# B's output weights in five pieces instead of seven, and the kept sums placed ahead of the last four rows

## The chip, the cores and the metric

The kernel runs on one core of one Trainium2 chip. The metric is the time of one execution on the device, in microseconds (us). Of the kernel before, three runs are shown: 1324.14 us is their median, 1324.11 the lowest and 1324.51 the highest. A profile of one more execution gives the trace that the text reads.

The engines are named as in the profile: PE is TensorE (PEld its weight loads), DVE is VectorE, ACT is ScalarE, POOL is GpSimd, SP is SyncE, which here issues nearly all DMAs. A name with a q (SPq, PEq) is that engine's sequencer.

## The reference

Two attention blocks, A and B, are computed for one new token of each of 2 sequences, and are mixed by a gate. Each has 32 heads of width 128 and a cache of 4096 keys and values for each head, all in float32; x is 2 x 512.

```python
def attend(x, k_cache, v_cache, wq, wo):             # once for A, once for B; both with A's x
    q = heads(x @ wq)                                # 512 -> 32 heads of 128
    p = softmax(einsum("bhqd,bhkd->bhqk", q, k_cache) * 128 ** -0.5)
    o = einsum("bhqk,bhkd->bhqd", p, v_cache)
    return flat(o) @ wo                              # 4096 -> 512
g = sigmoid((x * gate_w).sum(-1, keepdims=True))
out = g * attend(A) + (1 - g) * attend(B)
```

Nearly all of the data are the four caches, 128 MB each, of which every byte is used once. The output weights `wo` are 8 MB for A and 8 MB for B.

## The kernel before, in words

**The long part.** The work is cut into 32 units (A and B, eight groups of four heads, two sequences). A unit is 8 MB of keys and 8 MB of values. VectorE multiplies keys by the query and sums (L392, L395), ScalarE takes the exponentials (L367), and TensorE multiplies them with the values into the PSUM tile `vp` (L371). Keys go to two tiles `kt0` and `kt1`, values to one tile `vt`. Each engine runs its own loop, and semaphores written by hand tie the loops together. SP issues the loads in a fixed order, each one when its tile has become free. This part isn't changed.

**The end.** Three tiles are used again there. The last values go to `kt0`. A's output weights go to `vt` when the values before them have been used (L248). B's output weights go to `kt1` when the last keys have been used (L251). In both, a partition holds 32 rows of 512 numbers (`OR` = 32 rows of 2 KB, so a row of all 128 partitions is 256 KB). Row r of the output product is one matmul of a 128 x 2 column of `on` (the weighted and gated heads) with a 128 x 512 row of the weights. 32 rows of A and 32 of B are summed.

**How the rows are summed.** Rows go round over four strips of the PSUM tile `most`: row r adds to partitions 32s and 32s + 1, with s = r % 4 (`project_out`, L460 to L468). So `most` holds four partial sums, a strip each. This is done for all rows of A and rows 0 to 23 of B (`EARLY` = 24). ScalarE then copies `most` to the SBUF tile `kept` (L582).

The last eight rows of B go another way (`project_last`, L478 to L481): each is cut into four column ranges of 128, one for each strip, and these four matmuls add into four PSUM banks (`qa0`, `qa1`, `vp`, `bank`). The four partial sums of `kept` are folded into the same four banks by four matmuls with the matrix `fold` (L586), which adds the strips up. Then each bank holds a finished quarter of the output. Two engines copy the quarters, and two DMAs store the halves (L593 to L601).

**The order.** TensorE works strictly in the order of the program: A's rows, B's rows 0 to 23, rows 24 to 27 in the strips, the fold, rows 28 and 29, row 30, row 31 in two halves. Before a row with which a piece of the weights begins it waits for that piece (`arrived`; each piece has a semaphore of its own). A weight row here is one program instruction and appears in the trace as two matmuls and two weight loads, two passes of a float32 product.

**The pieces.** B's output weights are loaded in seven DMAs, on SP's queue one behind the other: rows 0 to 15, 16 to 23, 24 to 27, 28 and 29, 30, and the two halves of row 31 (L252, L253).

Of the kernel before, what the change touches and what calls it, by code (L numbers as in the profile page):

```python
# [13 lines left out]
B = 2  # L14
# [13 lines left out]
STRIPS = P // QT  # L28
OR = H * DH // P
DQ = DH // OR  # L30
EARLY = OR - 8
PAD = 72
NP = 2 * NG
SCALE = DH ** -0.5
# [13 lines left out]
class Streams:  # L48
# [32 lines left out]
    def put(self, e, make, reads=(), writes=(), gives=None):  # L81

        self.before(e, reads, writes)
        i = make(self.engines[e])
        if gives is not None:
            i.then_inc(gives, 1)
            return None
        self.ticks[e] += 1
        i.then_inc(self.sems[e], 1)
        point = self.sems[e], self.ticks[e]  # L90
        self.after(point, reads, writes)
        return point
# [51 lines left out]
def tile_gated_decode(ctx: ExitStack, tc: tile.TileContext, ins: dict, out: bass.AP):  # L144
# [14 lines left out]
    fold = small.tile([P, B], F32, name="fold")  # L159
# [22 lines left out]
    with tc.tile_critical(no_gpsimd_drain=True):  # L182
        S = Streams(nc, tc)
        put, take = S.put, S.take
# [26 lines left out]
        def load_parts(item, t, src, slots, *cuts):  # L211
            parts[item] = [S.dma("sp", t[:, i:j], src[:, i:j], slot=s) for s, i, j in zip(slots, cuts, cuts[1:])]

        def arrived(e, item, *which):
            p = parts[item]
            S.wait(e, [p[k] for k in which] if which else p)
# [27 lines left out]
        def load_wo(n):  # L244
            t = wo[n]
            src = ins[n + "_wo"].rearrange("(p r) e -> p r e", p=P)
            if n == "A":
                nc.sync.wait_ge(v_free, NU - 1)  # L248
                load_parts(("wo", n), t, src, "f", 0, OR)
                return  # L250
            nc.sync.wait_ge(k_free[1], NU // 2)  # L251
            load_parts(("wo", n), t, src, "abchi", 0, OR // 2, EARLY, OR - 4, OR - 2, OR - 1)  # L252
            parts["wo", n] += [S.dma("sp", t[:, OR - 1, h], src[:, OR - 1, h], slot=s) for s, h in zip("jk", HALVES)]  # L253

        wo = {n: t.rearrange("p r d -> p (r d)").rearrange("p (r e) -> p r e", e=D) for n, t in (("A", vt), ("B", kt[1]))}
# [10 lines left out]
        start = Scratch(kt[1]).take  # L266
# [191 lines left out]


        def project_out(k, n, *rows_):  # L460
            bounds = (0,) if n == "A" else (0, OR // 2)
            for r in range(*rows_):
                if r in bounds:
                    arrived("pe", ("wo", n), bounds.index(r))
                s = r % STRIPS
                put("pe", lambda x: x.matmul(most[s * QT:s * QT + B], on[:, k, r], wo[n][:, r],  # L466
                                             start=n == "A" and r < STRIPS, stop=n == "B" and r >= EARLY - STRIPS),
                    [r_on], [r_most])  # L468
# [5 lines left out]
        def strips(*which):  # L474
            for s in which or range(STRIPS):
                yield s, r_acc[s], acc[s][s * QT:s * QT + B, :W], slice(s * W, (s + 1) * W)

        def project_last(part, r, *which):  # L478
            arrived("pe", ("wo", "B"), part)
            for _, a, t, e_ in strips(*which):  # L480
                put("pe", lambda x: x.matmul(t, on[:, 1, r], wo["B"][:, r, e_], start=r == EARLY, stop=r == OR - 1), [r_on], [a])  # L481


        projections()
# [24 lines left out]
        for u in range(2, NU):  # L509
            load_k(u)  # L510
            load_v(u - 1)
        load_v(NU - 1)
        load_wo("A")
        load_wo("B")

        exps(0, 0, 0, lambda make, gives: put("act", make, [r_nm[0], r_sc, r_pad, r_lp, r_nil], [], gives))
# [16 lines left out]
        sums, turned, laid, outs, kept = end(2 * B * P), end(D), end(P), end(P), end(D)  # L533
        drawn, onp = end(D), end(2 * OR * B)
        on = onp.rearrange("p (n r b) -> p n r b", n=2, b=B)
        totals = [end(D // 2)[:B] for _ in HALVES]
        r_sums, r_drawn, r_turned, r_laid, r_outs, r_kept = R(), R(), R(), [R() for _ in range(2 * B)], R(), R()
# [8 lines left out]
        for j in range(STRIPS):  # L546
# [3 lines left out]
                start=True, stop=True), [r_pick, r_vs], [r_heads])  # L550
# [27 lines left out]
        r_on.writers = [point]  # L578

        project_out(0, "A", OR)  # L580
        project_out(1, "B", EARLY)
        put("act", lambda x: x.activation(kept, most, AF.Copy), [r_most], [r_kept])  # L582
        for r in range(EARLY, OR - 4):
            project_last(2, r)
        for _, a, t, e_ in strips():
            put("pe", lambda x: x.matmul(t, fold, kept[:, e_], start=False, stop=False), [r_fold, r_kept], [a])  # L586
        for r in range(OR - 4, OR - 2):
            project_last(3, r)
        project_last(4, OR - 2)
        project_last(5, OR - 1, 0, 1)  # L590
        project_last(6, OR - 1, 2, 3)

        for h, e in enumerate(("sp", "act")):  # L593
            copied, r_total = sem(f"copied{h}"), R()
            for i in range(2):
                _, a, t, _ = next(strips(2 * h + i))
# [28 lines left out]
```

## Time and profile before

| | |
|---|---|
| median of the runs shown (lowest to highest) | 1324.14 us (1324.11 to 1324.51) |
| span of the profiled execution, first to last instruction | 1322.3 us |
| DVE busy | 1165.3 us, 88% |
| PE busy | 331.7 us, 25% |
| ACT busy | 100.7 us, 8% |
| read from HBM, mean rate over the span | 570.43 MB, 431 GB/s |
| B's output weights: issue of the seven pieces begins | 1276.14 us |
| last matmul begins | 1319.23 us |

The runs' own time for the profiled execution is not listed beside its span. The span leaves out what lies ahead of the first instruction and behind the last, and the median of the runs is 1.8 us above it. Times in the text such as 1309.28 are us from the span's start. The matmuls' ends are modelled by the profiler. A timeline row gives start, duration, engine, line, operation, out and in, a count of merged instructions, and in brackets the idle time before and what ended it. In a row of a DMA the last number is the time from its issue to its landing. The granted clock (PEclk) is the share of TensorE's full clock that the chip's throttle let through.

### The profile page before, as it was taken

To read this page: it belongs to the slowest core of one execution; us is meant where nothing else is said; L and a number is where in the kernel's file an instruction comes from. 1 tells how busy PE (TensorE), PEld (TensorE's weight loads), DVE (VectorE), ACT (ScalarE), POOL (GpSimd) and SP (SyncE) were. 2 spreads that over 40 slices of the span, in tenths; PEclk is the share of its full clock that TensorE was granted. 3 is DMA by queue.
4 is the path that set the end of the run, shared out by engine and by line. 5 is a ranking of instruction groups with operands and counts; after the bars stand their busy time and mean duration, and the time that the engine had idled before them with its cause. 6 is when DMAs were issued, how large, how long until landed. Compare 5 with 4: busy or idle time off the path is not lost. (4 is left out here: it accounts for less than half of the span.)

```text
span 1322.3 us, 6216 instructions
## 1 busy us (share of the span) xinstructions
PE 331.7 (25%) x2382; PEld 90.3 (7%) x2382; DVE 1165.3 (88%) x316; ACT 100.7 (8%) x328; POOL 0.7 (0%) x6
## 2 busy tenths in 40 slices
PE   3112222211222221122222122222212322311256
PEld 0000000000000000000000000000000000000011
DVE  1978999999999999999999999999999999999961
ACT  0000100001010000101000010100001010000100
POOL 0000000000000000000000000000000000000000
PEclk9566666556666655666665666666556666555678
DMA  9999999999999999999999999999999999999998
GB/s 404 453 412 443 442 416 442 442 416 442 442 418 442 440 436 424 442 440 418 442 440 418 442 442 416 442 442 424 436 442 436 422 442 440 418 442 442 417 442 352
DMA packets 10820, 570.51 MB, mean 431 GB/s; under 512 B 1207, under 2 KB 1467, under 8 KB 1726
## 3 DMA queue, kind: packets, MB, share of 16 engines
q1 hardware_dynamic: 10804, 570.43, 99.6%
q8 instruction: 3, 0.05, 0.0%
q14 instruction: 3, 0.02, 0.0%
q10 hardware_dynamic: 10, 0.01, 0.0%
HBM read 570.43 MB, written 0.00 MB: 431 GB/s over the span
## 5 line engine op out<-in xcount | busy, mean ns | idle before, releaser
L392 DVE TENSOR_TENSOR kt<-kt,q 128x16384 f32<-128x16384 f32 x31 | 534.0, 17226 | 71.3 <-DVEq L97 71.3
L395 DVE TENSOR_REDUCE sc<-kt 128x128 f32<-128x16384 f32 x31 | 533.8, 17220 | 1.1
L371 PE MATMUL vp<-vt,pr 128*32 128x512 f32 x1984 | 283.1, 734 | 915.5 <-PEq L97 915.5
L371 PEld LDWEIGHTS vp<-vt,pr 128*32 128x32 f32 x1984 | 77.9, 132 | 1120.7 <-issue 1120.7
L367 ACT ACTIVATE pr<-sc,nm 32x128 f32<-32x128 f32 x128 | 50.9, 398 | 108.1 <-ACTq L97 102.8
L430 ACT ACTIVATE pr<-nil 128x512 f32<-128x512 f32 x31 | 19.3, 623 | 456.8 <-ACTq L97 456.8
L451 ACT ACTIVATE vs<-vp,slot 128x128 f32 x15 | 5.5, 368 | 448.1 <-ACTq L97 448.1
L337 PE MATMUL qa<-vt,cols 128*2 128x512 f32 x128 | 18.4, 739 | 39.9 <-PEq L97 39.9
L367 ACT ACTIVATION_READ_ACCUMULATOR pr<-sc,nm (+1 forms) x128 | 23.5, 184 | 0.0
L416 DVE SCALAR_TENSOR_TENSOR vs<-vp,slot,vs 128x128 f32 x45 | 15.8, 351 | 8.6 <-DVEq L97 7.6
L599 DVE COPY kt<-qa 2x128 f32<-2x128 f32 x1 | 0.3, 278 | 23.8 <-PE qa L481 23.8
L352 DVE STREAM_TRANSPOSE vt<-vt 128x1024 f32<-128x1024 f32 x2 | 2.4, 1224 | 17.1 <-ACT vt L348 17.1
L498 DVE TENSOR_REDUCE sc<-kt 128x64 f32<-128x8192 f32 x2 | 17.4, 8686 | 0.1
L496 DVE TENSOR_TENSOR kt<-kt,q 128x8192 f32<-128x8192 f32 x2 | 17.4, 8688 | 0.0
L455 ACT ACTIVATE vp<-nil 128x512 f32<-128x512 f32 x15 | 9.0, 600 | 99.2 <-ACTq L97 99.2
L544 DVE SCALAR_TENSOR_TENSOR vs<-vp,slot,vs 128x128 f32<-128x128 f32 x3 | 1.1, 351 | 12.9 <-ACT vs L542 12.8
L371 PE MATMUL vp<-kt,pr 128*32 128x512 f32 x64 | 9.0, 724 | 10.9 <-DMA kt<-in_B_v_cache_dram 10.9
L466 PE MATMUL most<-vt,kt 128*2 128x512 f32 x64 | 9.6, 765 | 6.5 <-DMA vt<-in_A_wo_dram 6.5
L400 DVE TENSOR_REDUCE rm<-sc 128x1 f32<-128x128 f32 x31 | 8.7, 281 | 2.3
L406 DVE STREAM_TRANSPOSE q<-qsel 128x128 f32<-128x128 f32 x30 | 9.3, 311 | 1.0
L289 DVE COPY cols<-bank 128x8 f32<-128x8 f32 x1 | 0.2, 167 | 10.0 <-PE bank L287 10.0
L401 DVE STREAM_TRANSPOSE across<-rm 128x32 f32<-128x32 f32 x31 | 6.6, 212 | 1.1
(73 smaller groups left out, 60.4 us busy)
## 6 DMA issues: line engine op xcount, KB each, us to landing
kt<-in_A_k_cache_dram SPq DMA_DIRECT2D x2, 4096.0 KB, 35.6
kt<-in_B_wo_dram SPq DMA_DIRECT2D x1, 4096.0 KB, 33.1
kt<-in_B_wo_dram SPq DMA_DIRECT2D x1, 2048.0 KB, 37.6
kt<-in_B_wo_dram SPq DMA_DIRECT2D x1, 1024.0 KB, 39.5
kt<-in_B_wo_dram SPq DMA_DIRECT2D x1, 512.0 KB, 40.3
vt<-in_A_v_cache_dram SPq DMA_DIRECT2D x16, 28.5
kt<-in_B_k_cache_dram SPq DMA_DIRECT2D x16, 42.6
kt<-in_B_wo_dram SPq DMA_DIRECT2D x1, 256.0 KB, 40.4
```

The source lines that it names most:

```text
L337: last = nc.tensor.matmul(t[h * QT:h * QT + B], cols[:, c], blocks[:, c, i, h], start=c == 0, stop=c == KC - 1)
L367: do(lambda x: x.activation(padded[h, :, b, j * VC:(j + 1) * VC], s[h].rearrange("p (c a) -> p c a", a=VC), AF.Exp, bias=m[h], accum_out=l ...
L371: return x.matmul(vp[c % STRIPS * QT:(c % STRIPS + 1) * QT], padded[:, c].rearrange("p b m -> p (b m)"), t[:, c * VC:(c + 1) * VC].rearran ...
L392: at = D_.do(lambda x: x.tensor_tensor(kt[o], kt[o], q[:, None, :].to_broadcast([P, NS, DH]), op=ALU.mult), after)
L395: at = D_.do(lambda x: x.tensor_reduce(sc[o], kt[o], axis=AX.X, op=ALU.add), at)
L406: return D_.do(lambda x: x.transpose(q, qsel[:, 0].to_broadcast([P, DH // QT, QT])), at)
L416: at = D_.do(lambda x: x.scalar_tensor_tensor(vs[:, g], vp[:, a * DH:(a + 1) * DH], slot[:, a:a + 1], vs[:, g], op0=ALU.mult, op1=ALU.add) ...
L430: return A_.do(lambda x: x.activation(padded[:, :, b], nil[:, :, None].to_broadcast([P, NVC, G * VC]), AF.Copy))
L455: A_.do(lambda x: x.activation(vp, nil.to_broadcast([P, VC * DH]), AF.Copy))
L466: put("pe", lambda x: x.matmul(most[s * QT:s * QT + B], on[:, k, r], wo[n][:, r], start=n == "A" and r < STRIPS, stop=n == "B" and r >= EA ...
L496: put("dve", lambda x: x.tensor_tensor(t, t, q[:, None, :].to_broadcast([P, NS // 2, DH]), op=ALU.mult), [r_q], [r])
L498: put("dve", lambda x: x.tensor_reduce(sc[0][:, h * NS // 2:(h + 1) * NS // 2], t, axis=AX.X, op=ALU.add), [r], [R()])
```

## The change

B's output weights come in five pieces: rows 0 to 21, rows 22 to 27, rows 28 to 30, and the two halves of row 31. Rows 0 to 27 of B, four more than before, go into `most`, and only the last four rows go into the strips. `kept` is folded into the four banks first, ahead of rows 28 to 31, and starts their sums (`start=True`), so the strip matmuls of the rows no longer start any. What is computed is the same.

```diff
-EARLY = OR - 8
+FIRST = OR - 10
+EARLY = OR - 4
@@ load_wo
-            load_parts(("wo", n), t, src, "abchi", 0, OR // 2, EARLY, OR - 4, OR - 2, OR - 1)
+            load_parts(("wo", n), t, src, "abc", 0, FIRST, EARLY, OR - 1)
             parts["wo", n] += [S.dma("sp", t[:, OR - 1, h], src[:, OR - 1, h], slot=s) for s, h in zip("jk", HALVES)]
@@ project_out
-            bounds = (0,) if n == "A" else (0, OR // 2)
+            bounds = (0,) if n == "A" else (0, FIRST)
@@ project_last
-                put("pe", lambda x: x.matmul(t, on[:, 1, r], wo["B"][:, r, e_], start=r == EARLY, stop=r == OR - 1), [r_on], [a])
+                put("pe", lambda x: x.matmul(t, on[:, 1, r], wo["B"][:, r, e_], start=False, stop=r == OR - 1), [r_on], [a])
@@ the end of the program
         project_out(0, "A", OR)
         project_out(1, "B", EARLY)
         put("act", lambda x: x.activation(kept, most, AF.Copy), [r_most], [r_kept])
-        for r in range(EARLY, OR - 4):
+        for _, a, t, e_ in strips():
+            put("pe", lambda x: x.matmul(t, fold, kept[:, e_], start=True, stop=False), [r_fold, r_kept], [a])
+        for r in range(EARLY, OR - 1):
             project_last(2, r)
-        for _, a, t, e_ in strips():
-            put("pe", lambda x: x.matmul(t, fold, kept[:, e_], start=False, stop=False), [r_fold, r_kept], [a])
-        for r in range(OR - 4, OR - 2):
-            project_last(3, r)
-        project_last(4, OR - 2)
-        project_last(5, OR - 1, 0, 1)
-        project_last(6, OR - 1, 2, 3)
+        project_last(3, OR - 1, 0, 1)
+        project_last(4, OR - 1, 2, 3)
```

Two places show how the order of instructions moves. Lines of the changed kernel are one higher up to its last loop (L466 becomes L467, L481 becomes L482), and the fold is L585. On TensorE, after A's rows, the kernel before has this; `kt_86` holds B's weights, `kt_85` holds `on` and `kept`, `landed_a` to `landed_c` are the semaphores of the first three pieces, and `done_act` is ScalarE's:

```order
L466 MATMUL most<-kt_86,kt_85 2x512 [waits landed_a]
L466 MATMUL most<-kt_86,kt_85 2x512 x15
L466 MATMUL most<-kt_86,kt_85 2x512 [waits landed_b]
L466 MATMUL most<-kt_86,kt_85 2x512 x7
L481 MATMUL qa_89<-kt_86,kt_85 2x128 [waits landed_c]
```

The changed kernel has there:

```order
L467 MATMUL most<-kt_86,kt_85 2x512 [waits landed_a]
L467 MATMUL most<-kt_86,kt_85 2x512 x21
L467 MATMUL most<-kt_86,kt_85 2x512 [waits landed_b]
L467 MATMUL most<-kt_86,kt_85 2x512 x5
L585 MATMUL qa_89<-kt_85,fold 2x128 [waits done_act]
```

Behind the first wait stand 22 rows instead of 16, and behind the last row into `most` comes a wait for ScalarE's copy instead of one for a piece of the weights. On SP's queue, behind A's output weights, the changed kernel has these loads of B's, and the store of the first half (sizes are partitions x numbers):

```order
L107 DMA vt<-in_A_wo_dram 128x16384
L107 DMA kt_86<-in_B_wo_dram 128x11264
L107 DMA kt_86<-in_B_wo_dram 128x3072
L107 DMA kt_86<-in_B_wo_dram 128x1536
L107 DMA kt_86<-in_B_wo_dram 128x256 x2
L107 DMA out_dram<-kt_85 2x256
```

Before, five loads of 8192, 4096, 2048, 1024 and 512 numbers stood in place of the three ahead of the two halves.

## The prediction

> **What bounds the kernel now.** I read the page first, then the DMA issues with their landings, then the last 25 us in order of time. The page's slices:
>
> ```profile
> span 1322.3 us, 6216 instructions
> PEclk9566666556666655666665666666556666555678
> DMA  9999999999999999999999999999999999999998
> DMA kt<-in_B_wo_dram 3%; DVE kt L392 1%; DVE sc L395 1%; PE qa L481 0%; SPq L106 0%; PE vp L481 0%; ACT kt L598 0%; PE qa L586 0%; PE bank L481 0%; DVEq L134 0%; PE bank L586 0%; PE vp L586 0%
> ```
>
> The DMA engines are busy in every slice, so the kernel ends when the last bytes have come and what hangs on them is done. The chain that ended last says the same of its last stretch: it is the load of B's output weights (3%), with some matmuls behind it. All that the change touches lies there. The loads and the issuing queue:
>
> ```profile
> kt<-in_B_wo_dram SPq DMA_DIRECT2D x1, 4096.0 KB, 33.1
> kt<-in_B_wo_dram SPq DMA_DIRECT2D x1, 2048.0 KB, 37.6
> kt<-in_B_wo_dram SPq DMA_DIRECT2D x1, 1024.0 KB, 39.5
> kt<-in_B_wo_dram SPq DMA_DIRECT2D x1, 512.0 KB, 40.3
> kt<-in_B_wo_dram SPq DMA_DIRECT2D x1, 256.0 KB, 40.4
> kt<-in_B_wo_dram SPq DMA_DIRECT2D x2, 128.0 KB, 39.9
> ```
> ```profile
> 1276.14 3.44 SPq L106 DMA_DIRECT2D kt<-in_B_wo_dram  x7
> ```
>
> The seven pieces are issued by 1279.6 and land from 1309.24 (1276.14 + 33.1) on. Now the end of the timeline, TensorE and ScalarE (start, duration, engine, line, operation, and in brackets the idle time before):
>
> ```profile
> 1299.47 9.58 PE L466 MATMUL most<-vt,kt 128*2 128x512 f32 x64 [6.49 <-DMA vt<-in_A_wo_dram]
> 1309.28 3.61 PE L466 MATMUL most<-kt,kt 128*2 128x512 f32 x32 [0.23 <-DMA kt<-in_B_wo_dram]
> 1314.13 1.90 PE L466 MATMUL most<-kt,kt 128*2 128x512 f32 x16 [1.23 <-DMA kt<-in_B_wo_dram]
> 1316.17 0.60 ACT L582 ACTIVATE kt<-most 128x512 f32<-128x512 f32 x1 [23.42 <-PE most L466]
> 1316.57 0.28 PE L481 MATMUL qa<-kt,kt 128*2 128x128 f32 x2 [0.55 <-DMA kt<-in_B_wo_dram]
> ...
> 1317.55 0.28 PE L586 MATMUL qa<-kt,fold 128*2 128x128 f32 x2
> ...
> 1319.11 0.09 PEld L481 LDWEIGHTS vp<-kt,kt 128*2 128x2 f32 x2 [0.30 <-DMA kt<-in_B_wo_dram]
> ...
> 1319.23 0.27 PE L481 MATMUL bank<-kt,kt 128*2 128x128 f32 x1
> ```
>
> At each piece TensorE is found waiting for a DMA, and after the last one (1319.11) only 0.39 us of matmuls follow, to 1319.50. The copy of `most` (L582, 0.60 us) lies wholly beside the wait for row 28 and the matmuls of rows 24 to 27. So the end is set by arrival: 16 rows take 9.81 us (1299.47 to 1309.28), the next 16, in six pieces, 9.83 (to 1319.11). That is 0.613 us a row, whatever the piece.
>
> **The price of a row on TensorE.** A row is one product, shown as two matmul records. Its pace is read from the weight loads, four in a group, two rows:
>
> ```profile
> 1300.28 0.15 PEld L466 LDWEIGHTS most<-vt,kt 128*2 128x2 f32 x4 [0.70 <-issue]
> 1301.14 0.15 PEld L466 LDWEIGHTS most<-vt,kt 128*2 128x2 f32 x4 [0.71 <-issue]
> ...
> 1305.02 0.10 PEld L466 LDWEIGHTS most<-vt,kt 128*2 128x2 f32 x4 [0.33 <-issue]
> 1305.45 0.10 PEld L466 LDWEIGHTS most<-vt,kt 128*2 128x2 f32 x4 [0.33 <-issue]
> ```
>
> 0.86 us for two rows early, 0.43 later: 0.43 and 0.214 us a row. The granted clock is the reason, seen in stretches of 3.4 us (columns: length; busy us of PE, PEld, DVE, ACT, POOL; granted clock; DMA):
>
> ```profile
> 1297.79:1301.19 3.40, 1.72 (x12) 0.31 (x16) 0.00 (x0) 0.00 (x0) 0.00 (x0) 0.50 0.92 390
> 1301.21:1304.60 3.39, 3.39 (x24) 0.56 (x20) 0.00 (x0) 0.00 (x0) 0.00 (x0) 0.50 0.92 396
> 1304.62:1308.02 3.40, 3.40 (x37) 0.73 (x32) 0.00 (x0) 0.00 (x0) 0.00 (x0) 1.00 1.01 434
> 1308.03:1311.43 3.40, 3.17 (x33) 0.62 (x29) 0.00 (x0) 0.00 (x0) 0.00 (x0) 1.00 0.98 419
> ...
> 178.23:181.62 3.39, 2.68 (x16) 0.82 (x20) 3.39 (x1) 0.00 (x0) 0.00 (x0) 0.50 1.11 483
> 181.64:185.03 3.39, 3.39 (x40) 1.02 (x36) 3.39 (x1) 0.00 (x0) 0.00 (x0) 1.00 0.98 425
> ...
> 1144.20:1147.60 3.40, 2.58 (x16) 0.73 (x20) 3.40 (x1) 0.00 (x0) 0.00 (x0) 0.50 0.76 328
> 1147.61:1151.00 3.39, 3.39 (x22) 0.88 (x18) 3.39 (x1) 0.00 (x0) 0.00 (x0) 0.50 1.34 580
> ...
> 727.77:731.17 3.40, 1.41 (x16) 0.21 (x8) 3.40 (x1) 0.63 (x1) 0.00 (x0) 1.00 0.89 386
> 731.18:734.58 3.40, 0.00 (x0) 0.00 (x0) 3.40 (x1) 0.00 (x0) 0.00 (x0) 1.00 0.76 328
> 734.60:738.00 3.40, 0.00 (x0) 0.00 (x0) 1.64 (x6) 1.69 (x7) 0.00 (x0) 0.50 1.34 578
> ...
> 843.82:847.22 3.40, 1.37 (x16) 0.17 (x8) 3.40 (x1) 0.89 (x2) 0.00 (x0) 1.00 0.80 347
> 847.24:850.64 3.40, 0.00 (x0) 0.00 (x0) 3.40 (x1) 0.00 (x0) 0.00 (x0) 0.50 0.76 328
> ```
>
> In these rows the clock changes only between windows of 3.41 us on a fixed grid. It is raised after a window with 2.68 us of matmuls or more, not after 2.58. It falls after one with 1.37 us or less, and is kept after 1.41.
>
> **The change, part by part.** *Fewer pieces.* Seven DMAs become five. Their issue (3.44 us for seven, so 0.5 each) ends 30 us before the first lands: nothing on the path. Nor do bytes come sooner: the last 16 rows in six pieces took 0.02 us longer than 16 rows in one. I bound this edit by -0.15 (all of the 0.30 us wait that the last half row shows, halved) and 0, and take 0.
>
> *The first piece has 22 rows.* It lands at the row pace at 1309.28 + 6/8 of the 4.85 us to 1314.13, so 1312.9. Until then TensorE, done with A at 1309.05, has nothing: 3.9 us idle instead of 0.23. Sixteen rows that were done at 1312.89 are now only begun.
>
> *Four more rows go to `most`.* At full clock 28 rows take 28 x 0.214 = 5.98 us, to 1318.9; with 0.19 us of drain (1.90 - 8 x 0.214) to 1319.1. The pieces of rows 22 to 27 (1316.6) and 28 to 30 (1318.4) have by then landed, or nearly.
>
> *The kept sums first.* The copy of `most` now stands between the 28 rows and the strips, whose first matmuls wait for it; rows 28 to 31 queue behind that wait, in order. Its cover is gone: 0.14 us to its start (1316.03 to 1316.17), 0.60, and some 0.06 to TensorE, so 0.80. Then five steps over the strips, of two passes each: ten passes ran from 1316.57 to 1317.55, 0.109 apart, so 9 x 0.109 + 0.27 = 1.25 us. End of the matmuls: 1319.07 + 0.80 + 1.25 = 1321.1, against 1319.50. Even at full clock that is **+1.6 us**; the copies and the store behind it stay as they are.
>
> *The clock.* The idle 3.9 us now meets the gate. With this execution's grid, the window 1308.03 to 1311.44 would hold matmuls only to 1309.05, 1.0 us, under 1.37: half clock from 1311.44. The 22 rows start at half. The window to 1314.86 has 1.95 us, too little; the next is full; full clock from 1318.27. So 5.4 us at half speed, costing half of that: +2.7, together **+4.3 us**. The grid need not fall so in another execution, so I bound it. Where the clock is at half when the rows start, the half-speed stretch lasts from 2.68 us to 2.68 + 3.41 = 6.09, which costs 1.3 to 3.0. Where the window around A's end still held 1.41 us, the fall comes up to 1.3 us into the rows, and then a whole window runs at half: 1.7. Moving the grid through 3.41 us in small steps and following these rules, the sum lies between +2.9 and +4.6, with its middle at +3.8, which I take.
>
> The Trainium skill, page "TensorE: Matmul & The Clock Gate", section "What's actually happening", lets the clock fall after at least one idle window of about 3.4 us. Taken to the letter, a gap of 3.9 us holds a whole idle window in only 0.5 of 3.41 positions, and mostly the clock would stay: +1.6. The trace disagrees: a window with 1.37 us of matmuls in it was enough (843.82).
>
> **From trace to run.** The sums are differences within an execution of 1322.3 us of span; the runs' median, 1324.14, has 1.8 us more outside it, which I carry over. +3.8 gives 1327.9.
>
> **Rivals.**
> 1. *The clock stays full over the gap.* +1.6, 1325.7. For it: 1312.89 to 1314.13 was bridged, and after 727.77 a whole empty window was. Against: it needs over 1.37 us of matmuls in every window around 3.9 us of nothing. 0.13.
> 2. *Arrival still sets the end,* as before, and the two saved pieces bring it forward: 1324.0, not slower. It decides if TensorE is done with 28 rows, copy and strips by 1319.5: (1319.5 - 1312.9 - 0.19 - 0.80 - 1.25) / 28 = 0.156 us a row. The quickest rows here take 0.214, in the sixteen that had all landed as well. 0.04.
> 3. *The clock never rises again before the end.* 28 rows at 0.43 instead of 0.214 cost 6.0, ten passes at 0.218 1.1: +8.7, 1332.8. It would need a window full of these matmuls that does not raise the clock; that of 1301.21 did. 0.03.
> 4. *The change does not do what it says.* The recorded order shows the 28 rows and the early kept sums, so this has no chance of its own.
>
> **How the numbers follow.** The forecast, half clock for part of the rows, has 0.80; it alone gives 1327.0 to 1328.8, with 0.2 either way for what I left at nothing. Rival 1 is next and lies below, so the range goes from 1325.6 to 1329.0. About 0.2% (2.65 us) is what a measurement of this kernel can tell from no change; the limit is 1326.8. The forecast's lower end comes within 0.3 of it, so I give 0.06 of its chance to no change, and with rival 1 and half of rival 2: slower 0.77, the same 0.21, faster 0.02.
>
> **What would show it.** Right: the group of `most` matmuls on B's weights has some 3.9 us of DMA wait in one piece before it and starts near 1312.9; the granted clock reads 0.50 in a stretch after that; the first strip matmul waits for ScalarE's copy of `most`; the chain's end runs through TensorE and that copy, with the last half row landed 2 us or more before its matmul. Runs whose grid lies otherwise differ by up to 1.7 us, more than the 0.4 of before. Wrong: 1.00 in all these windows (rival 1), a first piece that lands well before 1312.9, or a last strip that still waits for a DMA (rival 2).

## The result, and the profile after

The changed kernel takes 1327.65 us (median of 8 runs, 1327.18 to 1328.36), the kernel before in the same session 1324.11 (8 runs, 1323.96 to 1324.51). The ratio is 1.0027 with a 95% interval of 1.0018 to 1.0036: 3.5 us slower. The profiled execution took 1327.85 us, of which its span is 1326.1, so 1.8 us lie outside the span, as before.

The page of the changed kernel: the span, and the chain that ended last, by line. It now runs through the products into `most` (L467) and ScalarE's copy of it (L583), which did not appear in it before:

```profile
span 1326.1 us, 6166 instructions
DMA kt<-in_B_wo_dram 3%; DVE kt L393 1%; DVE sc L396 1%; PE most L467 1%; PE qa L482 0%; ACT kt L583 0%; ACT kt L596 0%; PE qa L585 0%; PE bank L482 0%; PE vp L482 0%; DVEq L135 0%; PE bank L585 0%; PE vp L585 0%
```

The loads of B's output weights, with KB and us from issue to landing:

```profile
kt<-in_B_wo_dram SPq DMA_DIRECT2D x1, 5632.0 KB, 36.6
kt<-in_B_wo_dram SPq DMA_DIRECT2D x1, 1536.0 KB, 39.9
kt<-in_B_wo_dram SPq DMA_DIRECT2D x1, 768.0 KB, 41.3
kt<-in_B_wo_dram SPq DMA_DIRECT2D x2, 128.0 KB, 41.0
```
```profile
1276.35 2.23 SPq L107 DMA_DIRECT2D kt<-in_B_wo_dram  x5
```

Issued from 1276.35 on, the first piece lands near 1312.95, and TensorE begins its rows at 1313.01. The timeline from A's rows to the store:

```profile
1299.69 8.72 PE L467 MATMUL most<-vt,kt 128*2 128x512 f32 x64 [5.64 <-DMA vt<-in_A_wo_dram]
1313.01 7.89 PE L467 MATMUL most<-kt,kt 128*2 128x512 f32 x56 [4.60 <-DMA kt<-in_B_wo_dram]
1321.04 0.60 ACT L583 ACTIVATE kt<-most 128x512 f32<-128x512 f32 x1 [27.23 <-PE most L467]
1321.69 0.28 PE L585 MATMUL qa<-kt,fold 128*2 128x128 f32 x2 [0.79 <-ACT kt L583]
...
1322.70 0.27 PE L482 MATMUL bank<-kt,kt 128*2 128x128 f32 x1
1322.98 0.28 DVE L597 COPY kt<-qa 2x128 f32<-2x128 f32 x1 [26.64 <-PE bank L482]
1323.03 0.27 ACT L596 ACTIVATE kt<-qa 2x128 f32<-2x128 f32 x1 [1.39 <-PE bank L482]
1323.29 0.28 DVE L597 COPY kt<-vp 2x128 f32<-2x128 f32 x1
1323.32 0.27 ACT L596 ACTIVATE kt<-bank 2x128 f32<-2x128 f32 x1
...
1323.62 0.26 ACTq L107 DMA_DIRECT2D out_dram<-kt  x1
```

TensorE waits 4.60 us for the 22-row piece, works without a pause through all 28 rows, waits 0.79 us for the copy, and ends at 1322.97 (1322.70 + 0.27). No matmul behind the first piece waits for a DMA any more: the two halves of row 31 have landed by 1319.6 (issued by 1278.58, 41.0 us), 3 us before their matmuls begin at 1322.57. The granted clock in the windows around the wait (length; busy us of PE, PEld, DVE, ACT, POOL; clock; DMA):

```profile
1309.96:1313.34 3.38, 0.33 (x4) 0.11 (x8) 0.00 (x0) 0.00 (x0) 0.00 (x0) 1.00 0.77 327
1313.37:1316.76 3.39, 3.39 (x20) 0.68 (x16) 0.00 (x0) 0.00 (x0) 0.00 (x0) 0.50 0.97 403
1316.79:1320.18 3.39, 3.39 (x36) 0.85 (x32) 0.00 (x0) 0.00 (x0) 0.00 (x0) 1.00 0.22 78
```

Here the rows begin at full clock. It falls 0.35 us later, behind a window that held 0.33 us of matmuls, and a whole window of 3.41 us runs at half, which costs 1.71.

The matmuls end 3.47 us later than before (1322.97 against 1319.50): 1.76 from the chain at full clock and 1.71 from the clock. The time of this execution lies 3.74 above the median of before (1327.85 against 1324.11), 0.27 more. The end of the kernel before shows where that comes from:

```profile
1319.13 0.28 DVE L599 COPY kt<-qa 2x128 f32<-2x128 f32 x1 [23.84 <-PE qa L481]
1319.17 0.27 ACT L598 ACTIVATE kt<-qa 2x128 f32<-2x128 f32 x1 [2.40 <-PE qa L481]
...
1319.53 0.28 DVE L599 COPY kt<-vp 2x128 f32<-2x128 f32 x1
1319.57 0.27 ACT L598 ACTIVATE kt<-bank 2x128 f32<-2x128 f32 x1
1319.87 0.26 ACTq L106 DMA_DIRECT2D out_dram<-kt  x1
```

Before, the first half of the output was copied (1319.13, 1319.17) while TensorE still worked on the second, and the last store was issued from 1319.87, 0.37 us behind the last matmul. Now all four strips end together, VectorE and ScalarE copy two quarters each one after the other, and the store is issued from 1323.62, 0.65 us behind: 0.28 more.

### The profile page after: what moved, and what is told of

Same layout as the page of the kernel before. It is cut to its first block, busy times and chain, and to the rows that moved or that the text cites. A ratio compares the mean times of both kernels' runs of the same rounds, so it can differ in the third digit from the quotient of the medians.

```text
span 1326.1 us, 6166 instructions
## 1 busy us (share of the span) xinstructions
PE 334.7 (25%) x2358; PEld 91.0 (7%) x2358; DVE 1165.3 (88%) x316; ACT 100.6 (8%) x328; POOL 0.7 (0%) x6
## 5 line engine op out<-in xcount | busy, mean ns | idle before, releaser
L467 PE MATMUL most<-vt,kt 128*2 128x512 f32 x64 | 8.7, 707 | 5.6 <-DMA vt<-in_A_wo_dram 5.6
L467 PE MATMUL most<-kt,kt 128*2 128x512 f32 x56 | 7.9, 726 | 4.6 <-DMA kt<-in_B_wo_dram 4.6
```

## The experiments

The theory has three parts: a 22-row piece makes TensorE start late (rows), the copy of `most` lost its cover (copy), and the wait lets the clock fall (clock). Against it stood that the clock has no part, that the loss lies in the new order alone, and that fewer pieces bring something. Times are medians; "before" is the kernel before, measured beside it on the same chip.

| run | runs | us | before | ratio (95%) |
|---|---|---|---|---|
| 16 extra products in the wait | 11 | 1325.94 (1325.78 to 1326.65) | 1324.04 | 1.0016 (1.0006 to 1.0025) |
| first piece split, 16 + 6 rows | 11 | 1325.31 (1325.06 to 1325.94) | 1324.04 | 1.0010 (1.0001 to 1.0019) |
| extra products, fold late | 11 | 1325.20 (1325.01 to 1325.56) | 1324.04 | 1.0010 (1.0000 to 1.0019) |
| before, rows 28 to 30 in one piece | 11 | 1324.16 (1323.97 to 1324.48) | 1324.04 | 1.0001 (0.9992 to 1.0010) |
| new order, pieces of before to row 27 | 12 | 1324.57 (1324.35 to 1324.97, and one run of 1334.58) | 1324.11 | 1.0011 (0.9999 to 1.0023) |
| first piece of 26 rows | 5 | 1330.35 (1329.81 to 1330.98) | 1324.11 | 1.0047 (1.0034 to 1.0060) |

**TensorE kept busy in the wait.** The changed kernel with 16 products between A's rows and B's, into a PSUM tile that nobody reads again:

```diff
         project_out(0, "A", OR)
+        for r in range(16):
+            s = r % STRIPS
+            put("pe", lambda x: x.matmul(heads[s * QT:s * QT + B], on[:, 0, r], wo["A"][:, r], start=True, stop=True),
+                [r_on], [r_heads])
```

> The changed kernel with 16 extra row products between A's rows and B's, into the PSUM tile of the heads, which nobody reads any more; they take 16 x 0.214 = 3.4 us of the 4 to 5 us in which TensorE waits for the 22-row piece, and end before it lands. Theory (1.9 of the 3.5 us come from the granted clock at half): the clock reads 1.00 from A's rows to the end, and the kernel takes before + 1.6 = 1325.7 us. Rival (the clock has no part, all 3.5 us are rows and copy behind a late piece): 1327.6, as the change.

The timeline, and one stretch from the start of B's rows to the last matmul:

```profile
1307.77 3.61 PE L584 MATMUL heads<-vt,kt 128*2 128x512 f32 x32
1313.15 6.19 PE L467 MATMUL most<-kt,kt 128*2 128x512 f32 x56 [1.77 <-DMA kt<-in_B_wo_dram]
```
```profile
1313.15:1321.40 8.25, 7.46 (x96) 2.31 (x96) 0.00 (x0) 0.60 (x1) 0.00 (x0) 1.00 0.54 217
```

More work made the kernel 1.7 us faster than the change (1325.94 against 1327.65). The clock reads 1.00 throughout, the 28 rows take 6.19 us instead of 7.89, and from their start to the last matmul's end it is 8.25 us; the prediction had 5.98 + 0.19 + 0.80 + 1.25 = 8.22. The rival falls: half of the loss is the clock. The 0.2 above the expected 1325.7 fit the 0.28 of the output's copies named above.

**The kept sums behind three rows.** As the run before, with the fold moved:

```diff
+        for r in range(EARLY, OR - 1):
+            project_last(2, r)
         for _, a, t, e_ in strips():
-            put("pe", lambda x: x.matmul(t, fold, kept[:, e_], start=True, stop=False), [r_fold, r_kept], [a])
-        for r in range(EARLY, OR - 1):
-            project_last(2, r)
+            put("pe", lambda x: x.matmul(t, fold, kept[:, e_], start=False, stop=False), [r_fold, r_kept], [a])
```

(and the first of these rows starts the sums, `start=r == EARLY`).

> As the run with 16 extra products, but the kept sums enter the strips behind rows 28 to 30 instead of ahead of them, so that these rows cover the copy of most. Theory: 0.65 us (three rows at 0.218) of the copy's 0.80 are hidden again: before + 0.95 = 1325.1 us, 0.6 less than the other run. Rival (the copy was hidden anyway, for instance behind landings): no difference between the two.

```profile
1312.81 6.19 PE L467 MATMUL most<-kt,kt 128*2 128x512 f32 x56
1319.14 0.60 ACT L587 ACTIVATE kt<-most 128x512 f32<-128x512 f32 x1 [26.04 <-PE most L467]
1319.79 0.09 PEld L591 LDWEIGHTS qa<-kt,fold 128*2 128x2 f32 x4 [0.43 <-ACT kt L587]
1319.79 0.28 PE L591 MATMUL qa<-kt,fold 128*2 128x128 f32 x2
```

The fold still begins 0.79 us behind the last row into `most` (1319.00 to 1319.79), released by the copy as in the change, but now three rows run in that time. TensorE stands still for only some 0.14 us of it (1319.65 to 1319.79). The median is 0.74 us less than the run with the fold early, and the two sets of runs do not overlap. From the start of B's rows to the last matmul's end (1320.41) it is 7.60 us instead of 8.25, just the 0.65 that three rows take. So the place of the fold alone cost the change 0.65 to 0.74.

**The first piece split.** The changed kernel, rows 0 to 15 and 16 to 21 as two pieces:

```diff
-            load_parts(("wo", n), t, src, "abc", 0, FIRST, EARLY, OR - 1)
+            load_parts(("wo", n), t, src, "ahbc", 0, OR // 2, FIRST, EARLY, OR - 1)
-            bounds = (0,) if n == "A" else (0, FIRST)
+            bounds = (0,) if n == "A" else (0, OR // 2, FIRST)
```

(Not shown: the numbers of the pieces that the last four rows wait for go up by one.)

> The changed kernel with one edit: the 22-row piece comes as two, rows 0 to 15 and 16 to 21 (six pieces). Theory (the late first piece is the cause): rows 0 to 15 run at 1309.3, rows 16 to 21 at 1313.0, rows 22 to 27 at 1316.6; the copy of most begins near 1318.0, the last matmul ends near 1320.1, +0.6 against before: 1324.7 us, up to 1325.3 where the clock falls in the 2.3 us wait ahead of rows 22 to 27. Rival (the loss is in the order of the fold and the four more rows): stays above 1326.5.

2.3 us of the 3.5 are gone with this one edit, so the late first piece causes two thirds of the loss, the fall of the clock included (it reads 1.00 here from the start of B's rows to the last matmul). The rival "the order" falls as the whole of the loss. But 1.27 us stay, not 0.6; the time given for a fallen clock, 1325.3, is met by chance, as the clock did not fall. 0.28 are the output's copies again. The rest is in this run's last rows into `most`, the products and their weight loads:

```profile
1316.48 1.89 PE L467 MATMUL most<-kt,kt 128*2 128x512 f32 x12 [1.75 <-DMA kt<-in_B_wo_dram]
```
```profile
1316.48 0.11 PEld L467 LDWEIGHTS most<-kt,kt 128*2 128x2 f32 x8 [2.68 <-DMA kt<-in_B_wo_dram]
1316.91 0.09 PEld L467 LDWEIGHTS most<-kt,kt 128*2 128x2 f32 x2 [0.32 <-issue]
1317.34 0.09 PEld L467 LDWEIGHTS most<-kt,kt 128*2 128x2 f32 x2 [0.34 <-issue]
```

The weight loads of eight rows in the kernel before, behind the first group (1314.13):

```profile
1314.56 0.10 PEld L466 LDWEIGHTS most<-kt,kt 128*2 128x2 f32 x4 [0.33 <-issue]
1314.99 0.10 PEld L466 LDWEIGHTS most<-kt,kt 128*2 128x2 f32 x4 [0.33 <-issue]
```

Six rows take 1.89 us, as long as the eight of the kernel before (1.90), at a clock of 1.00; six times 0.214 and the drain would be 1.47. Rows 22 to 27 begin with strips 2 and 3, so they touch two of the strips twice. The trace fits a price by rounds: four strips run side by side for 0.86 us, and a strip's second row needs a second round, full or not (the later groups hold two weight loads instead of four, at the same spacing of 0.43). No other run tests this. That is 0.42 us more than expected, and 0.6 + 0.28 + 0.42 = 1.3.

**The new order with early pieces.** The changed kernel's order, with pieces 0 to 15, 16 to 23, 24 to 27, 28 to 30, and two halves:

```diff
-            load_parts(("wo", n), t, src, "abc", 0, FIRST, EARLY, OR - 1)
+            load_parts(("wo", n), t, src, "ahbc", 0, OR // 2, OR - 8, EARLY, OR - 1)
-            bounds = (0,) if n == "A" else (0, FIRST)
+            bounds = (0,) if n == "A" else (0, OR // 2, OR - 8)
```

(Not shown: the numbers of the pieces that the last four rows wait for go up by one here too.)

> The changed kernel with its order of matmuls (28 rows into most, kept sums first), but the pieces of before up to row 27: rows 0 to 15, 16 to 23, 24 to 27, then 28 to 30 and two halves. Theory (the order alone costs next to nothing when pieces arrive as before): rows 24 to 27 run from 1316.6 to 1317.4, the copy ends at 1318.4, fold and rows 28 to 30 end by 1319.3, behind the landing of the first half row but with the last at 1319.1: last matmul ends at 1319.7, before + 0.2, 1324.3 us. Rival (the lost cover of the copy, 0.8 us, shows in full): 1324.9.

```profile
1309.07 3.61 PE L467 MATMUL most<-kt,kt 128*2 128x512 f32 x32 [1.10 <-DMA kt<-in_B_wo_dram]
1316.34 1.04 PE L467 MATMUL most<-kt,kt 128*2 128x512 f32 x8 [0.53 <-DMA kt<-in_B_wo_dram]
1317.53 0.60 ACT L583 ACTIVATE kt<-most 128x512 f32<-128x512 f32 x1 [24.16 <-PE most L467]
1318.18 0.28 PE L585 MATMUL qa<-kt,fold 128*2 128x128 f32 x2 [0.79 <-ACT kt L583]
```

Measured +0.46, between the two expectations, with an interval that just takes in no change. The matmuls end at 1319.45, where the theory had 1319.7; but the pieces come sooner in this execution, the first by 0.21 us (1309.07 against 1309.28). From the first row of B to the last matmul's end it is 10.38 us, before it was 10.22 (1309.28 to 1319.50): 0.16 more, close to the 0.2 of the theory, and the copies one after the other add 0.28. Behind row 24 no matmul waits for a DMA any more: copy, fold and last rows set the end. The order costs little where the pieces land early, because this chain then ends hardly later than the last landing would have let it. One of the twelve runs took 1334.58 us, at a mean clock of 0.527 where the others read 0.63; why is open, and without it the median is 1324.56.

**Fewer pieces alone.** The kernel before, rows 28 to 30 in one piece:

```diff
-            load_parts(("wo", n), t, src, "abchi", 0, OR // 2, EARLY, OR - 4, OR - 2, OR - 1)
+            load_parts(("wo", n), t, src, "abch", 0, OR // 2, EARLY, OR - 4, OR - 1)
```

(Not shown: rows 28 to 30 wait for this one piece, and the numbers of the pieces behind it go down by one.)

> The kernel before with one edit: rows 28 to 30 come in one piece instead of two (six pieces), the order of the matmuls unchanged. Theory (pieces cost nothing as such): same time as before, 1324.1 us, within 0.15, the last half row landing within 0.1 us of before. Rival (each piece costs something at the end): 0.15 us less or better.

+0.12, with an interval of about 1 us either way: no gain that can be seen, and an effect of 0.15 could not have been told apart by time. The profiles can say a little: the last matmul ends at 1319.31 with A's weights ready at 1299.24, so 20.07 us later; before it was 1319.50 - 1299.47 = 20.03. Row 30 is there 9.10 us after the first piece (1309.15 to 1318.25), before it was 9.14 (1309.28 to 1318.42). Row 31 doesn't wait in this run, so its landing can't be read. All four strips end together here too, and the last store is issued from 1319.96, 0.65 us behind the last matmul, as in the change: a small gain could be hidden behind that.

**A later first piece.** The changed kernel with `FIRST = OR - 6`, so 26 rows in the first piece and 2 in the second.

> The changed kernel with a first piece of 26 rows and a second of 2. Theory: it lands 4 x 0.61 = 2.45 us later, near 1315.4; the wait is some 7 us, so the clock is at half whenever it ends, for 2.7 to 6.1 us, which costs 1.3 to 3.0. Sum: 1.6 + 2.45 + 1.3 to 3.0 = before + 5.4 to 7.1, 1329.5 to 1331.2 us, middle 1330.3. Rival (the arrival of the first piece doesn't set the start of the rows): 1327.6, as the change.

```profile
1315.02 4.45 PE L467 MATMUL most<-kt,kt 128*2 128x512 f32 x20 [7.09 <-DMA kt<-in_B_wo_dram]
```
```profile
1309.65:1313.04 3.39, 0.00 (x0) 0.00 (x0) 0.00 (x0) 0.00 (x0) 0.00 (x0) 1.00 0.74 321
1313.07:1316.45 3.38, 1.43 (x8) 0.25 (x12) 0.00 (x0) 0.00 (x0) 0.00 (x0) 0.50 0.93 379
1316.48:1319.86 3.38, 3.38 (x20) 0.59 (x16) 0.00 (x0) 0.00 (x0) 0.00 (x0) 0.50 0.21 75
1319.90:1323.28 3.38, 3.38 (x36) 0.67 (x28) 0.00 (x0) 0.00 (x0) 0.00 (x0) 1.00 0.00 0
```

+6.2 us, in the middle of the expected 5.4 to 7.1. The rows start at half clock; the window to 1316.46 holds 1.43 us of them, too little, so a second one follows at half.

**Six more profiles of the changed kernel.** Nothing is edited; only the windows of the clock lie elsewhere. Two came first, four later. The sum is used as the second text gives it, with the start of B's rows for the landing:

> The changed kernel once more, for another position of the clock's windows. Theory: the half-speed stretch within B's rows begins and ends on windows of 3.41 us; the last matmul ends at its value at full clock, 3.6 us less than the landing of the first piece counted as 1312.9 + 8.2 = 1321.1, plus half the length of the stretch that lies within the rows. Rival: the end moves without regard to that stretch.

> The same, for a third position: the end of the last matmul is the landing of the first piece + 8.2 us + half the time that the rows of B run at a granted clock of 0.50. Rival: no such relation.

> The changed kernel once more, one of four looks at where the clock's windows of 3.41 us lie. In the ten profiled executions so far (of all kernels here) a window began between 1301.2 and 1303.1 us of the span. Theory one (any position is as likely as another): a look falls outside that stretch with a chance of 1.5 in 3.4, so some two of the four do. Theory two (the position hangs together with the program's start): all four fall inside. In each, the last matmul ends at the start of B's rows + 8.2 us + half of the half-speed time within them.

> The second of the four looks, as the first: outside 1301.2 to 1303.1 in two of four where any position is as likely, inside in all where it hangs on the program's start.

> The third of the four looks, as the first: outside 1301.2 to 1303.1 in two of four by theory one, inside in all by theory two.

> The fourth of the four looks, as the first: outside 1301.2 to 1303.1 in two of four by theory one, inside in all by theory two.

The half-speed time is read from where the granted clock changes; the calculated end is the start of B's rows + 8.22 + half of that time.

| execution | B's rows start | half speed within them | calculated end | last matmul ends | time, us |
|---|---|---|---|---|---|
| 16 extra products | 1313.15 | 0 | 1321.37 | 1321.40 | 1326.31 |
| the change, first profile | 1313.01 | 3.41 | 1322.94 | 1322.97 | 1327.85 |
| second | 1312.68 | 2.99 | 1322.40 | 1322.40 | 1327.28 |
| third | 1313.04 | 3.42 | 1322.97 | 1322.99 | 1328.01 |
| fourth | 1312.85 | 3.22 | 1322.68 | 1322.69 | 1327.57 |
| fifth | 1313.24 | 2.95 | 1322.94 | 1322.94 | 1327.82 |
| sixth | 1313.12 | 5.17 | 1323.93 | 1323.93 | 1328.81 |
| seventh | 1312.63 | 3.42 | 1322.56 | 1322.58 | 1327.46 |
| first piece of 26 rows | 1315.02 | 4.86 | 1325.67 | 1325.67 | 1330.55 |

Nine executions, and the sum holds within 0.03 us in each. The rival (no relation) falls. In the sixth the windows lie as in the profile of before, on which the prediction's +4.3 was worked out; its matmuls end at +4.43, and the 0.1 more is the later start of its rows (1313.12 against 1312.9, of which half is made up by a shorter time at half speed):

```profile
1299.58 9.53 PE L467 MATMUL most<-vt,kt 128*2 128x512 f32 x64 [6.53 <-DMA vt<-in_A_wo_dram]
1313.12 3.59 PE L467 MATMUL most<-kt,kt 128*2 128x512 f32 x16 [4.01 <-DMA kt<-in_B_wo_dram]
```
```profile
1308.08:1311.44 3.36, 1.03 (x12) 0.10 (x4) 0.00 (x0) 0.00 (x0) 0.00 (x0) 1.00 0.81 351
1311.49:1314.85 3.36, 1.73 (x12) 0.32 (x16) 0.00 (x0) 0.00 (x0) 0.00 (x0) 0.50 0.95 404
1314.90:1318.27 3.37, 3.37 (x24) 0.55 (x20) 0.00 (x0) 0.00 (x0) 0.00 (x0) 0.50 0.83 332
1318.31:1321.68 3.37, 3.37 (x36) 0.62 (x28) 0.00 (x0) 0.00 (x0) 0.00 (x0) 1.00 0.02 6
```

Where the windows lie stays open: a window began between 1301.2 and 1303.1 in three of the last four executions and at 1303.43 in the other. Neither theory's count (two outside, none outside) came out.

## Why the prediction was right

It gave 1327.9 us in a range of 1325.6 to 1329.0, and slower; measured were 1327.65, slower, with the whole interval above no change. All executions of the changed kernel, the eight runs and the six more, lie between 1327.18 and 1328.81, a spread of 1.6 where the prediction had up to 1.7.

- **Arrival set the end before, TensorE sets it now.** Right. Rival 2 (arrival still sets it) falls by the change's own timeline, where no matmul behind the first piece waits for a DMA.
- **The first piece lands at 1312.9.** Right: some 1312.95, and the rows began between 1312.63 and 1313.24 in seven executions.
- **28 rows at 0.214 us, the drain, the copy's lost cover, five steps over the strips: +1.6 at full clock.** Right: 8.25 us measured at full clock against 8.22, and most of the copy's share shown by moving the fold (0.65 to 0.74). In the first profile it is 1.76, as its rows begin 0.1 later than 1312.9.
- **The clock: half speed for 2.7 to 6.1 us.** Right in mechanism and size: 2.95 to 5.17 us in seven executions of the change. Rival 1 (the clock stays full) falls. Only with work put into the wait did the clock stay full there; then 1325.94 stands beside the 1325.7 given for it. Rival 3 (it never rises) was not seen in any execution.
- **The clock's rule by windows.** The prediction read from the trace of before that a window with 1.37 us of matmuls or less is enough to lose the full clock, and the changed kernel shows it where it matters: in the sixth execution the clock was at half from 1311.46, behind a window with 1.03 us, and in the first profile behind one with 0.33. The Trainium skill, page "TensorE: Matmul & The Clock Gate", section "What's actually happening", asks for at least one idle window. Here no window lay wholly within the 4.01 us of waiting, and by the letter of that section the clock would have stayed at full; the measurement decides against the letter.
- **"the copies and the store behind it stay as they are" was wrong,** a term left at nothing that measures 0.28 us: the copies of the first half had run beside the wait for the last half row, and lost that cover as the copy of `most` did. It shows in every run in which the strips end together.
- **The middle over the windows' positions was 0.5 too high.** +3.8 is the middle between the ends +2.9 and +4.6, not a mean over positions. By an estimate with the prediction's own rules and times, evenly spaced positions give a mean of 3.5 to 3.6; the most frequent value is 3.3 (one whole window at half), and in about one position in twenty the clock stays full. The eight runs' median (+3.54) less the copies is +3.26. The two errors, 0.54 too much and 0.28 too little, partly cancelled. That the forecast came within 0.25 us is in part luck, and no measure of how good the sum was.
- **Fewer pieces at nothing** agrees with the runs, but is not shown to better than about 1 us.

No version here is shown to be faster than the kernel before. Of those in the new order the one with early pieces comes nearest (1324.57), and its end is set by the copy, the fold and the last rows.

## What to carry to other kernels

A piece of a load is also a start signal: every row merged into the first one delays all work behind it. That work has to fit between the first landing and the last; here 8.22 us stood against the 6.2 between 1312.9 and the last wait of before, 1319.11. Merging some of the last pieces alone (rows 28 to 30) changed nothing that could be seen. A wait of 4 to 5 us in TensorE's stream was priced twice here, once as idle time and once as half-clock time after it, and independent products in the gap paid for themselves. When a chain end moves, ask of each small copy behind it what it used to run beside.

## What the hardware showed that was not expected

- Float32 rows with two stationary columns, spread over four strips of PSUM partitions, seem to cost by rounds of four: four rows took 1.04 us, six 1.89, eight 1.90, each with about 0.19 of drain (six rows were seen in one execution only). In a long run of rows this reads as 0.214 a row and hides the rounding.
- Sixteen useless products made the kernel 1.7 us faster than without them, as the text ahead of that run had forecast.
- In fourteen profiled executions of all kernels here, the clock's windows began at positions that cover only 1301.2 to 1303.4, of the 3.4 us in which they could lie. Whether the position hangs on the program's start isn't settled.
